# The lead-in of a lightning-attention and FFN kernel: both v cast by their transfers, w_in in other pieces, and the last block in three column pieces

## The chip, the cores and the metric

The kernel runs on one core of a Trainium2 chip. The metric is the device time of one execution in microseconds (us); the time of a version is the median of several executions. The engines are PE (matrix multiply, with PEld for its weight loads), DVE, ACT and POOL for element work, and SP, which issues transfers; POOL and ACT issue transfers too. The transfers run on 16 DMA engines that all queues share. PE writes to PSUM, 8 banks; DVE and ACT copy from there to SBUF.

## The reference

Decayed linear attention in blocks of 64 rows over (batch 4, heads 8, sequence 768, head size 64), and its output, as 3072 rows of 512, through a feed-forward part with g = h cos(h):

```python
for b in range(nb):
    intra = np.einsum('bhic,bhjc->bhij', qb, kb) * Dmask[None]
    intra = np.einsum('bhij,bhjd->bhid', intra, vb)
    inter = np.einsum('bhid,bhde->bhie', qb * lam_pow[None], kv_state)
    out[:, :, sl] = intra + inter
    kv_state = lam_block[None, :, None, None] * kv_state + np.einsum('bhsd,bhse->bhde', kb_dec, vb)
x = attn_out.transpose(0, 2, 1, 3).reshape(B * S, H * D)
h = x @ w_in             # 512 x 2048
out = (h * np.cos(h)) @ w_out   # 2048 x 512
```

Inputs and output are float32; the kernel multiplies in bf16.

## The kernel before

The 3072 rows are 24 blocks of 128 rows, taken in pairs, and grouped into tiles of the feed-forward part (`TILES`, line 21: 4, 2, 2, 2, 2, 2, 2, 4, 4 blocks). For each tile PE computes h by 16 column blocks f of 128 (`hidden`, line 702, matmuls at L705 into `ps_h`), ACT takes the cosine (L711), DVE multiplies (`gated`, L717) into `g`, and PE projects with w_out by groups of four f (`project`, L748 into `ps_f`); ACT copies the result (`project_out`, L762) and SP stores it (`store_out`, L769 and L771).

The attention of a tile is worked into the feed-forward part of the tile before. Only tile 0 has none before it: its four blocks are the **spans**, two stretches of 256 rows (x = 0 and 1), and their attention is the lead-in. `add_span` (line 545) makes it: q and k of a span are scaled (L559), transposed on PE (L570) and copied to SBUF by ACT (L573); scores on PE (L581), masked on DVE (L586); `update` (L595) makes the state between the span's two 128-row chunks, `update_out` (L599) copies it into `kv_bd`; `values` (L608) and `carried` (L614) make the output, which `values_out` (L622) copies into `xT`, the left operand of the first h. The masked scores come in two halves of heads (hp = 0 and 1).

Loads: `add_span_load` (line 272) brings q, k and v of a span. q and k come by SP as float32. v of span 0 comes by POOL's queue, whose transfers can change the type, so it arrives as bf16; it is issued once k of span 0 has landed. v of span 1 comes by SP as float32, once k of span 1 has landed, and POOL and ACT cast half of it each (`cast_v`, L563). The weights come by POOL's queue too, cast by their transfers: w_in in four pieces of 3, 5, 4 and 4 column blocks f (`W_IN`, line 37), then w_out in four pieces of four. `ORDER` (line 35) names the order; transfers of one queue are issued in it. The second w_in piece waits for the scaling of span 1's k, the fourth for the casts. The first loads of the blocks of tile 1 (q4 and on) wait on SP for the third w_out piece.

The order of all instructions on each engine comes from a planner (line 54): a greedy list schedule of tasks with durations, latencies, priorities and PSUM banks that are written at each task. At each step it takes the task that can start first, and among those on one engine the smallest priority. Its outcome is the fixed order of each engine's instructions, so an engine whose next instruction waits does nothing else meanwhile. In tile 0 the first `SPLIT` column blocks f (3) are done in two halves of 256 rows, so that h can begin on span 0 while span 1 is not ready; a task of the planner before `lead_end` is preceded by filler matmuls (`keep_awake`, L826) for the time that the plan shows PE idle.

The last block's projection (line 735) is done in two pieces of 256 columns; the first is copied by DVE and stored by SP, the second copied and stored by ACT.

Of the kernel before, what the change touches and what calls it, by code (L numbers as in the profile page):

```python
# [10 lines left out]
F32 = mybir.dt.float32  # L11
# [7 lines left out]
SPANS = 2  # L19
DMA_FROM = 6  # L20
TILES = [4, 2, 2, 2, 2, 2, 2, 4, 4]
SPLIT = 3
# [9 lines left out]
VALUES_OUT = [[("ACT",), ("ACT",)], [("ACT", "DVE"), ("ACT", "DVE")]]  # L32
STATE_OUT = [("ACT", "DVE"), ("ACT", "DVE")]
LATE = 30.0
ORDER = "q0 k0 q1 k1 v0 v1 i0 i1 i2 i3 o0 o1 o2 o3"

W_IN = [3, 5, 4, 4]
# [104 lines left out]
def kernel(  # L142
# [10 lines left out]
    nc = tc.nc  # L153
    B, H, S, D = q.shape
    P = 128
# [17 lines left out]
    BUFS = {"ld": 6, "qk": 3, "v_s": 6, "qkT": 3, "s_m": 4, "cos": 3, "o_sb": 3}  # L173
# [98 lines left out]
    def add_span_load(name, src, x, prio, deps):  # L272
        def emit(_):
            if on_pool:
                t = span_v[x]
            else:
                if ("raw", x) not in live:
                    live["raw", x] = work.tile([P, 3, H, 2, D], F32, tag="g", name="sp_f")
                t = live[name, "sp", x] = live["raw", x][:, "qkv".index(name[0])]
            return start(nc.gpsimd if on_pool else nc.sync, t.rearrange("u h s d -> u h (s d)"),  # L280
                         src[x, :, 0:2 * P, :].rearrange("h (u s) d -> u h (s d)", s=2), deps)

        on_pool = name == "v_f" and x == 0
        issue, load_t[name, "sp", x] = dma("POOL" if on_pool else "SP", 1.5, 1.0 if on_pool else 0.5, emit, prio, deps,
                                           lat=0.7 if name == "v_f" and x else 1.0)
        return load_t[name, "sp", x]
# [14 lines left out]
    def add_w(which, c, prio, deps=()):  # L301
        def emit(_):
            if which == "in":
                a, z = sum(W_IN[:c]) * P, sum(W_IN[:c + 1]) * P
                return start(nc.gpsimd, w_in_sb[:, :, a:z], w_in_src[:, :, a:z], deps)
            a, z = c * KF // WCH, (c + 1) * KF // WCH
            return start(nc.gpsimd, w_out_sb[:, a:z, :], w_out_src[:, a:z, :], deps)

        part = W_IN[c] / 4 if which == "in" else 1.0
        early = which == "in" and c < 2  # L310
        _, w_t[which, c] = dma("POOL", 2.68 * part, 0.8, emit, (-2000.0 if c == 0 else -997.5) if early else prio, deps,
                               lat=2.4 if early and c == 0 else 1.2)
        return w_t[which, c]
# [231 lines left out]
    def add_span(x):  # L545
# [16 lines left out]
        def cast_v(_, hp):  # L562
            (nc.scalar.copy if hp else nc.gpsimd.tensor_copy)(span_v[x][:, cut[hp]], live["v_f", "sp", x][:, cut[hp]])  # L563

# [24 lines left out]
        def update(t):  # L589
            kv_ps = L["kv"] = bank(t.bank[0], [P, NP, D], F32, "ps_kv")  # L590
            rows = chunks[0][0]
            for p in range(NP):
                for s in range(2):
                    for i, h in enumerate(halves):
                        nc.tensor.matmul(kv_ps[h, p, :], lhsT=L["k"][rows, s, 2 * p + i, :], rhs=L["v"][rows, s, 2 * p + i, :],  # L595
                                         start=(p == 0 and s == 0), stop=True, skip_group_check=True)

        def update_out(_, h, e):
            (nc.scalar.copy if e == "ACT" else nc.vector.tensor_copy)(kv_bd[h, x, :, h], L["kv"][h])  # L599
# [18 lines left out]
        def values_out(_, c, e, pairs):  # L618
            if ("xT", 0) not in live:
                live["xT", 0] = work.tile([P, KD, 4 * P], BF16, tag="xT", name="xT")  # L620
            n = 2 * x + c
            (nc.scalar.copy if e == "ACT" else nc.vector.tensor_copy)(  # L622
                live["xT", 0][:, pairs, n * P:(n + 1) * P], L["o"][c][:, pairs])

        so, kt, v_t = [[], []], [], [[load_t["v_f", "sp", x]]] * 2
        if x:

            v_t = [[pl.add(("POOL", "ACT")[hp], 0.61, [load_t["v_f", "sp", x]], partial(cast_v, hp=hp), pa(-1.0 + 0.1 * hp))] for hp in range(2)]
            w_t["in", 3].issue.deps += v_t[0] + v_t[1]
            late = w_t["in", 1].issue  # L630
        for hp in range(2):
# [3 lines left out]
            if x:  # L635
                late.deps.append(kt[hp])
            outs = []
            for name, src in (("qT", a), ("kT", kt[hp])):
                e = OUTS[x][name][hp]
                t = pl.add("PE", MM(P, 4), [src], partial(transposes, name=name, hp=hp), pa(-0.5 + 0.1 * hp), banks=1)  # L640
                if x and name == "kT" and hp == 0:
                    spans[0]["update"].deps.append(t)
                outs.append(pl.add(e, 0.58 if e == "ACT" else 0.42, [t], partial(transposes_out, name=name, hp=hp, e=e), pa(-0.5 + 0.1 * hp)))
                t.bank_frees = [[outs[-1]]]
            s1 = pl.add("PE", 0.42, outs, partial(scores, hp=hp), pa(0.1 + 0.1 * hp), banks=2)
            so[hp] = [pl.add("DVE", 0.69, [s1], partial(scores_out, hp=hp, i=i), pa(0.1 + 0.1 * hp + 0.05 * i)) for i in range(2)]
            s1.bank_frees = [[t] for t in so[hp]]

        u = pl.add("PE", 0.42, v_t[0] + v_t[1] + kt, update, pv(0.1), banks=1)
        L["update"] = u  # L650
        Uo_sp[x] = [pl.add(e, 0.4 if e == "ACT" else 0.42, [u], partial(update_out, h=h, e=e), pv(0.1))
                    for h, e in zip(halves, STATE_OUT[x])]
        u.bank_frees = [Uo_sp[x]]
        span_deps.extend(v_t[0] + v_t[1] + kt)
        v0 = pl.add("PE", 0.35, so[0] + v_t[0], partial(values, hp=0), pv(0.2), banks=2)
        v1 = pl.add("PE", 0.35, [v0] + so[1] + v_t[1], partial(values, hp=1), pv(0.25))
        second = pl.add("PE", MM(P, 4) + 0.1, [v1] + Uo_sp[x], carried, pv(0.3))
        for c, (t, by) in enumerate(zip((v1, second), VALUES_OUT[x])):
            cuts = [slice(i * NP // len(by), (i + 1) * NP // len(by)) for i in range(len(by))]
            Vo[2 * x + c] = [pl.add(e, 0.16 + 0.44 / len(by), [t], partial(values_out, c=c, e=e, pairs=pairs), pv(0.3) if c == 0 else -1200.0)  # L660
                             for e, pairs in zip(by, cuts)]
        v0.bank_frees = [Vo[2 * x], Vo[2 * x + 1]]

# [25 lines left out]
    def add_ffn(i):  # L689
# [43 lines left out]
        for j in range(nb):  # L733
            last = n0 + j == NBLK - 1
            pieces = [slice(0, DM // 2), slice(DM // 2, DM)] if last else [slice(0, DM)]
            store = None
            for piece, part in enumerate(pieces):
# [36 lines left out]
                eng, queue = ("DVE", "SP") if last and piece == 0 else ("ACT", "ACT" if last else "SP")  # L774
                e = pl.add(eng, 0.12 + width / 1060.0, [store], partial(project_out, eng=eng), begins[i + 1] + (j + 1) * nxt / nb,
                           get="o_sb")
                d = dma(queue, 1.2 if n0 + j < 2 * SPANS else 0.9, 1.7 if n0 + j < 2 * SPANS else 0.75, partial(store_out, eng=queue), n0 + j + 8, [e], ordered=False)[1]
# [9 lines left out]
    for at, name in enumerate(names):  # L787
# [5 lines left out]
        elif n < SPANS and at < 9:  # L793
            kept.append(add_span_load(which + "_f", src[which], n, at - 2040, {"v0": kept[1:2], "v1": kept[3:4]}.get(name, [])))
        else:
            kept.append(add_load(n, which + "_f", src[which], at, deps))
# [69 lines left out]
```

## Time and profile before

| | us |
|---|---|
| median of 5 executions | 208.92 (208.65 to 209.33) |
| the profiled execution | 208.77 |
| its span, first to last instruction | 207.1 |
| PE busy | 199.7 (96% of the span) |
| PE's granted clock, mean | 1.000 |
| DVE, ACT, POOL busy | 114.4, 119.0, 63.3 |
| v of span 0: issued, landed | 7.33, 12.5 |
| first w_in piece: issued, to landing | 8.40, 6.2 |
| v of span 1: issued, landed | 10.11, 16.1 |
| first h matmul | 15.60 |
| h without a break from | 19.98 |
| last ps_f matmul starts | 203.2 |
| last copy (ACT, 128x256) ends | 203.97 |

Times in the profile count from the first instruction. A row of a timeline or of the chain gives the start, the length, the engine, the line of the code and the operation, written as output<-inputs; "idle before <-" says how long the engine had been idle and what ended that. The chain of waits is followed back from the last instruction to what released it, so it shows what set the end, piece by piece. SPq, POOLq and ACTq rows are issues of transfers; their data moves later. What lies between the span and the execution's time (1.67 us) is outside the program's instructions.

### The profile page before, as it was taken

To read this page: it belongs to the slowest core of one execution; us is meant where nothing else is said; L and a number is where in the kernel's file an instruction comes from. 1 tells how busy PE (TensorE), PEld (TensorE's weight loads), DVE (VectorE), ACT (ScalarE), POOL (GpSimd) and SP (SyncE) were. 2 spreads that over 40 slices of the span, in tenths; PEclk is the share of its full clock that TensorE was granted. 3 is DMA by queue.
4 is the path that set the end of the run, shared out by engine and by line. 5 is a ranking of instruction groups with operands and counts; after the bars stand their busy time and mean duration, and the time that the engine had idled before them with its cause. 6 is when DMAs were issued, how large, how long until landed. Compare 5 with 4: busy or idle time off the path is not lost.

```text
span 207.1 us, 5989 instructions
## 1 busy us (share of the span) xinstructions
PE 199.7 (96%) x2498; PEld 117.6 (57%) x2498; DVE 114.4 (55%) x222; ACT 119.0 (57%) x231; POOL 63.3 (31%) x83
## 2 busy tenths in 40 slices
PE   6988999999999999999999999999999999999993
PEld 2456544555846857667667766655454444444462
DVE  2876686275972956647476664745784444444000
ACT  5865773233946867566659486746766555354120
POOL 4368001275055261546372363526200000000000
PEclk9999999999999999999999999999999999999999
DMA  4999999997889998999999999999500110111112
GB/s 126 293 218 199 208 206 200 215 258 182 191 200 208 216 247 207 225 184 260 225 251 156 225 232 218 207 205 247 131 3 3 51 51 0 54 51 51 51 77 75
DMA packets 95706, 34.20 MB, mean 165 GB/s; under 512 B 83264, under 2 KB 92736, under 8 KB 95680
## 3 DMA queue, kind: packets, MB, share of 16 engines
q1 hardware_dynamic: 90272, 29.24, 64.4%
q0 software_dynamic: 5264, 4.46, 13.7%
q8 instruction: 19, 0.31, 0.7%
q10 hardware_dynamic: 144, 0.13, 0.2%
q14 instruction: 7, 0.06, 0.1%
HBM read 27.27 MB, written 6.29 MB: 162 GB/s over the span
## 4 chain that ended last, share of the span: by engine, by line
PE 88%; DMA 6%; SPq 2%; DVE 1%; issue 1%; ACT 1%; POOL 0%; ACTq 0%
PE ps_h L705 40%; PE ps_f L748 40%; DMA sp_f<-in_v_dram 3%; DMA sp_f<-in_k_dram 3%; PE ps_o L475 2%; PE ps_kv L426 2%; PE ps_s L414 1%; PE ps_o L503 1%; SPq L266 1%; DVE v_s L344 1%; PE ps_t L366 0%; DVE xT L622 0%; ACT xT L622 0%; DVE qkT L369 0%; PE ps_o L608 0%
## 5 line engine op out<-in xcount | busy, mean ns | idle before, releaser
L717 DVE TENSOR_TENSOR g<-ps_h,cos 128x256 bf16<-128x256 f32 (+1 forms) x147 | 73.0, 506 | 57.7 <-ACT cos L711 57.0
L711 ACT ACTIVATE cos<-ps_h,halfpi 128x256 f32<-128x256 f32 (+1 forms) x147 | 75.4, 540 | 36.3 <-PE ps_h L705 36.1
L748 PE MATMUL ps_f<-w_out_sb,g 128*128 128x512 bf16 (+1 forms) x400 | 92.8, 371 | 0.0
L705 PE MATMUL ps_h<-xT,w_in_sb 128*128 128x256 bf16 (+1 forms) x588 | 92.4, 305 | 0.2 <-ACT xT L622 0.2
L705 PEld LDWEIGHTS <-w_in_sb 128*128 128x128 bf16 x588 | 57.1, 98 | 32.4 <-DVE xT L511 0.4
L748 PEld LDWEIGHTS <-g 128*128 128x128 bf16 x400 | 38.0, 98 | 35.7
L336 POOL TENSOR_TENSOR qk<-q_f,q_scale 128x512 bf16<-128x512 f32 x19 | 19.9, 1066 | 41.1 <-DMA q_f<-in_q_dram 31.3
L344 POOL TENSOR_TENSOR v_s<-v_f,v_scale 128x512 bf16<-128x512 f32 x19 | 19.6, 1042 | 16.2 <-DMA v_f<-in_v_dram 14.9
L762 ACT COPY o_sb<-ps_f 128x512 f32<-128x512 f32 (+1 forms) x24 | 13.9, 577 | 17.9 <-PE ps_f L748 17.5
L511 ACT CAST xT<-ps_o 128x512 bf16<-128x512 f32 x19 | 10.2, 588 | 15.6 <-PE ps_o L503 14.0
L419 DVE TENSOR_TENSOR s_m<-ps_s,mask 128x512 bf16<-128x512 f32 x20 | 12.9, 684 | 1.0 <-PE ps_s L414 0.7
L340 POOL CAST qk<-k_f 128x512 bf16<-128x512 f32 x18 | 11.0, 612 | 4.9 <-DMA k_f<-in_k_dram 4.7
L826 PE MATMUL ps_idle<-blank,ident 128*128 128x512 bf16 (+2 forms) x30 | 9.8, 457 | 1.6 <-POOL ident masks.py:199 1.6
L432 DVE TENSOR_TENSOR sum<-sum,ps_kv 128x512 f32<-128x512 f32 x15 | 10.2, 681 | 0.6
L437 ACT CAST S<-sum 128x512 bf16<-128x512 f32 x15 | 9.1, 619 | 2.5 <-DVE sum L432 2.4
L475 PEld LDWEIGHTS <-v_s 64*64 64x64 bf16 x320 | 4.2, 107 | 4.8 <-issue 4.6
L475 PE MATMUL ps_o<-s_m,v_s 64*64 64x64 bf16 x320 | 6.4, 197 | 0.5
L762 DVE COPY o_sb<-ps_f 128x256 f32<-128x256 f32 x1 | 0.4, 426 | 10.8 <-PE ps_f L748 10.8
L826 PEld LDWEIGHTS <-ident 128*128 128x128 bf16 x30 | 3.1, 116 | 4.8 <-issue 2.5
L586 DVE TENSOR_TENSOR s_m_sp<-ps_s,mask_sp 128x512 bf16<-128x512 f32 x8 | 5.0, 683 | 0.1
L426 PE MATMUL ps_kv<-v_s,qk 64*64 64x64 bf16 x288 | 4.8, 194 | 0.1
L340 ACT CAST qk<-k_f 128x512 bf16<-128x512 f32 x2 | 1.2, 618 | 6.3 <-DMA k_f<-in_k_dram 6.3
(71 smaller groups left out, 78.9 us busy)
## 6 DMA issues: line engine op xcount, KB each, us to landing
q_f<-in_q_dram SPq DMA_DIRECT2D x20, 256.0 KB, 4.2
k_f<-in_k_dram SPq DMA_DIRECT2D x20, 256.0 KB, 4.3
v_f<-in_v_dram SPq DMA_DIRECT2D x20, 256.0 KB, 4.6
out_dram<-o_sb SPq DMA_DIRECT2D x19, 256.0 KB, 2.6
w_out_sb<-in_moe_w_out_dram POOLq DMA_DIRECT2D x4, 512.0 KB, 13.5
out_dram<-o_sb SPq DMA_DIRECT2D x9, 128.0 KB, 2.4
sp_f<-in_q_dram SPq DMA_DIRECT2D x2, 512.0 KB, 5.3
sp_f<-in_k_dram SPq DMA_DIRECT2D x2, 512.0 KB, 5.6
```

Of the source, the lines that this page charges most:

```text
L336: vec[e].tensor_mul(new_qk()[:, 0, :, s], live.pop(("q_f", 2 * pr + s)), q_scale[:, c, :].unsqueeze(2).to_broadcast([P, H, D]))
L340: (nc.scalar.copy if early else nc.gpsimd.tensor_copy)(new_qk()[:, 1, :, s], live.pop(("k_f", 2 * pr + s)))
L344: vec[e].tensor_mul(live["v_s", 2 * pr + s], live.pop(("v_f", 2 * pr + s)), v_scale[:, c, :].unsqueeze(2).to_broadcast([P, H, D]))
L419: nc.vector.tensor_mul(t, live["s", pr][s], mask.unsqueeze(1).to_broadcast([P, H, D]))
L432: nc.vector.tensor_add(new, live["sum", pr, 0] if half else live["sum", pr - 1, 1], live["kv", pr][half])
L475: yield lambda h=h: nc.tensor.matmul(o[halves[h % 2], h // 2, m], lhsT=live["v_s", n0 + s][m, h, :], rhs=live["s_m", n0 + s][m, h, :], sta ...
L705: nc.tensor.matmul(t[:, :n], lhsT=w_in_sb[:, kd, f * P:(f + 1) * P], rhs=live["xT", i][:, kd, at], start=(kd == 0), stop=(kd == KD - 1))
L711: nc.scalar.activation(c[:, :n], live["h", i, f, at.start][:, :n], AF.Sin, bias=halfpi)
L717: nc.vector.tensor_mul(live["g", i][:, f, at], live.pop(("h", i, f, at.start))[:, :n], live.pop(("c", i, f, at.start))[:, :n])
L748: nc.tensor.matmul(live["f", i, j, piece][:, :width], lhsT=live["g", i][:, f, j * P:(j + 1) * P], rhs=w_out_sb[:, f, part], start=(f == 0) ...
L762: (nc.scalar.copy if eng == "ACT" else nc.vector.tensor_copy)(o[:, :width], live["f", i, j, piece][:, :width])
L826: nc.tensor.matmul(idle_ps[:, :n], lhsT=ident, rhs=blank[:, :n], start=True, stop=True)
```

## The change

Seven edits come together.

1. v of span 1 comes as v of span 0 does: by POOL's queue, cast by its transfer, without a wait of its own, in order behind v of span 0 and ahead of w_in. `cast_v` is gone, and the wait of a w_in piece for it.
2. w_in comes in five pieces of 2, 2, 4, 4 and 4 column blocks; the second still waits for the scaling of span 1's k.
3. `update` and the first `values` of span 0 stand behind span 1's first scores (before, `update` behind the transposes of its k).
4. `update` writes the two halves of heads into two PSUM banks; span 0's state is copied by ACT alone, span 1's by ACT and DVE. A chunk of span 1's output is copied whole, one by ACT and one by DVE, instead of each in two halves by both.
5. `SPLIT` is 4, and the planner's latencies of the early transfers are other numbers, so the whole plan is made anew.
6. The stores of tile 0 get a lower priority on SP, and there are four buffers `o_sb` instead of three.
7. The last block is projected in columns of 256, 128 and 128; the first two are copied by DVE and stored by SP.

```diff
-SPLIT = 3
+SPLIT = 4
-VALUES_OUT = [[("ACT",), ("ACT",)], [("ACT", "DVE"), ("ACT", "DVE")]]
-STATE_OUT = [("ACT", "DVE"), ("ACT", "DVE")]
+VALUES_OUT = [("ACT", "ACT"), ("ACT", "DVE")]
+STATE_OUT = [("ACT", "ACT"), ("ACT", "DVE")]
-ORDER = "q0 k0 q1 k1 v0 v1 i0 i1 i2 i3 o0 o1 o2 o3"
-W_IN = [3, 5, 4, 4]
+ORDER = "q0 k0 q1 k1 v0 v1 i0 i1 i2 i3 i4 o0 o1 o2 o3"
+W_IN = [2, 2, 4, 4, 4]
...
-    BUFS = {"ld": 6, "qk": 3, "v_s": 6, "qkT": 3, "s_m": 4, "cos": 3, "o_sb": 3}
+    BUFS = {"ld": 6, "qk": 3, "v_s": 6, "qkT": 3, "s_m": 4, "cos": 3, "o_sb": 4}
...
-        on_pool = name == "v_f" and x == 0
+        on_pool = name == "v_f"
         issue, load_t[name, "sp", x] = dma("POOL" if on_pool else "SP", 1.5, 1.0 if on_pool else 0.5, emit, prio, deps,
-                                           lat=0.7 if name == "v_f" and x else 1.0)
+                                           lat=1.6 if on_pool else 1.0)
...
-                               lat=2.4 if early and c == 0 else 1.2)
+                               lat=1.9 if early else 1.2)
...
-        def cast_v(_, hp):
-            (nc.scalar.copy if hp else nc.gpsimd.tensor_copy)(span_v[x][:, cut[hp]], live["v_f", "sp", x][:, cut[hp]])
...
-            kv_ps = L["kv"] = bank(t.bank[0], [P, NP, D], F32, "ps_kv")
+            L["kv"] = [bank(i, [P, NP, D], F32, "ps_kv") for i in t.bank]
...
-            w_t["in", 3].issue.deps += v_t[0] + v_t[1]
...
-                if x and name == "kT" and hp == 0:
-                    spans[0]["update"].deps.append(t)
...
+            if x and hp == 0:
+
+                for t in spans[0]["late"]:
+                    t.deps.append(s1)
...
-        u = pl.add("PE", 0.42, v_t[0] + v_t[1] + kt, update, pv(0.1), banks=1)
+        u = pl.add("PE", 0.42, v_t + kt, update, pv(0.1), banks=2)
...
+        L["late"] = [u, v0]
...
-            pieces = [slice(0, DM // 2), slice(DM // 2, DM)] if last else [slice(0, DM)]
+            cuts = [0, DM // 2, 3 * DM // 4, DM] if last else [0, DM]
+            pieces = [slice(a, z) for a, z in zip(cuts, cuts[1:])]
...
-                eng, queue = ("DVE", "SP") if last and piece == 0 else ("ACT", "ACT" if last else "SP")
+                eng, queue = ("DVE", "SP") if last and piece < 2 else ("ACT", "ACT" if last else "SP")
...
-                d = dma(queue, 1.2 if n0 + j < 2 * SPANS else 0.9, 1.7 if n0 + j < 2 * SPANS else 0.75, partial(store_out, eng=queue), n0 + j + 8, [e], ordered=False)[1]
+                d = dma(queue, 1.2 if n0 + j < 2 * SPANS else 0.9, 1.7 if n0 + j < 2 * SPANS else 0.75, partial(store_out, eng=queue), n0 + j + (26.5 if n0 + j < 2 * SPANS else 8), [e], ordered=False)[1]
...
-            kept.append(add_span_load(which + "_f", src[which], n, at - 2040, {"v0": kept[1:2], "v1": kept[3:4]}.get(name, [])))
+            kept.append(add_span_load(which + "_f", src[which], n, at - 2040, kept[1:2] if name == "v0" else []))
```

## The prediction, on record before the result

> **What bounds the kernel now.** I read four views in this order. First the busy table and the 40 slices of the page: PE is busy 96% of 207.1 us and its granted clock is full in every slice, so time is won only where PE is idle, does filler, or where the end comes after its last matmul. Second the chain of waits that ended last, in order of time (start, length, what):
>
> ```profile
> 4.11 5.98 DMA sp_f<-in_k_dram
> 10.11 6.01 DMA sp_f<-in_v_dram
> 16.11 0.06 issue
> 16.17 0.62 POOL v_sp L563
> ...
> 18.70 0.83 DVE xT L622 x2
> 19.55 0.38 ACT xT L622
> 19.98 12.69 PE ps_h L705 x64
> 32.67 0.63 PE ps_kv L672 x32
> 33.30 7.01 PE ps_f L748 x32
> 40.31 0.45 PE ps_t L366 x8
> ...
> 45.10 0.04 issue
> 45.15 0.44 PE ps_kv L426 x30
> ...
> 189.66 13.87 PE ps_f L748 x80
> 203.59 0.37 ACT o_sb L762
> ```
>
> The second span's v sets the lead-in: it lands at 16.11, is cast, goes through PE and leaves PSUM as xT at 19.92. From 19.98 to 203.6 the chain is PE nearly without a hole (0.6 us idle between 34 and 190 in the table by stages). A microsecond gained in the lead-in arrives at the end only if no later wait takes its place.
>
> Third the order of time of POOL's and SP's queues, and SP's waits:
>
> ```profile
> 7.33 1.08 POOL L266 DMA_DIRECT2D v_sp<-in_v_dram  x1 [3.67 <-DMA sp_f<-in_k_dram]
> 8.40 0.78 POOL L266 DMA_DIRECT2D w_in_sb<-in_moe_w_in_dram  x1
> 38.54 1.04 POOL L336 TENSOR_TENSOR qk<-q_f,q_scale 128x512 bf16<-128x512 f32 x1 [3.83 <-DMA q_f<-in_q_dram]
> SPq L266 <- DMA w_out_sb<-in_moe_w_out_dram: 22.9, 1, 22.9
> ```
>
> The last line matters most: the loads of tile 1 (q4 and on) wait on SP for the third w_out piece, which lands at 33.34. So the weights' stream on POOL's queue dates both the weights and tile 1's loads.
>
> Fourth the packet records and landings of the DMA engines. Landings in us: k1 10.09, v0 12.51, w_in 0 14.56, v1 16.11, w_in 1 to 3 20.63, 23.18, 25.78, w_out 28.31, 30.81, 33.34, 35.94. The engines served these in order of issue: v1, issued on SP at 10.11, has no packet before 13.7, when w_in 0 is nearly through. From 9 to 36 us they are never free, so a place gained by one transfer is lost by another.
>
> **The transfers after the change.** v0 stays (12.51). v1 is issued behind it at 8.4 on POOL, without waiting. It has 1024 packets that write 256 B, as v0; v0's went at 440 per us, so 2.33 us: last packet at 12.23+2.33=14.56, landing 0.28 later, **14.84** instead of 16.11. The two casts (L563, 0.61 us) go too: v1 is usable 1.9 us sooner. The price: as f32 by SP its 1024 packets went at 678 per us, 1.51 us, so the stream is 0.8 us longer.
>
> w_in 0 and 1 are now two column blocks each: 512 packets that write 512 B, which no row shows. Neighbours: 256 B 36 ns per packet and engine, 768 B 67 ns, 1024 B 80 ns. I take the middle, 52 ns (bounds 36 and 67): 32 packets per engine, 1.66 us (1.16 to 2.13). w_in 0 lands at **16.5** (16.0 to 17.0), two us later than now; w_in 1 at 18.2 (17.2 to 19.1). One more term: during w_in 1 the 16 engines' landings spread from 0.8 to 1.95 us, one of them carrying a 16 KB instruction packet of 0.95 us. Nothing says where this falls now: 0 to 1.2 us, I take 0.3, so w_in 1 at **18.5**. Each further piece is 2.53 us (distance of the landings above): w_in 2 at 21.0, third w_out piece at 33.7, 0.35 later than now (bounds 32.4 to 35.5).
>
> POOL: v0 1.08, v1 1.08, w_in 0 0.78 from 7.33 ends at 10.27; the k preps behind started at 10.26 (k1 lands at 10.09). Nothing. w_in 1 and later are issued from 12.3 as now; the two later ones no longer wait for the casts (16.72), but their descriptors queue behind earlier pieces anyway: nothing.
>
> **PE in the lead-in.** Second span's scores first: update and values of span 0 now stand behind scores that need POOL's k prep (11.34), transposes and an ACT copy (0.58), so they start near 13.0 instead of 12.55. Costs nothing: what follows waits for v1 and w_in. It frees DVE earlier: the masked scores of span 1 end near 15.6 instead of 16.42. Both halves of span 0's state on ACT add 0.37 there; xT of span 0 is ready near 15.3 (now 15.22), covered by w_in 0 at 16.5. Two banks let ACT and DVE copy span 1's state side by side (now 17.39 then 17.77, 0.4 saved), also before w_in 0: nothing by itself.
>
> So w_in sets the pace. By the planner's order of earliest starts the h of f0 and f1 for blocks 0 and 1 come ahead of the last values of span 1, so PE idles from about 15.5 to 16.5, does these 8 matmuls (0.109 each, rows at 15.6: 0.87), values and carried (0.6, to 18.1), and xT's last chunk leaves on DVE near 19.0 (0.69 row at L511). Then f2, f3 on w_in 1: 18.5+0.87 (with SPLIT 4 four f are cut in halves); the four second halves 16 x 0.109=1.74, to 21.1, when w_in 2 (21.0) is there; 48 matmuls of 512 columns x 0.216=10.37, to **31.5**. The same sum for before, 19.98 + 12 x 0.109 + 52 x 0.216, gives 32.5 where the chain shows 32.67; with that 0.1 the h phase ends at 31.6, **1.1 us sooner**. Bounds: 1.45 sooner (xT at 19.05 is then the limit) to 0.75 later (w_in 1 at 20.3).
>
> The idle microsecond on PE: the trace's first matmuls of 512 columns are 427 ns apart, from 1.6 to 6 us, and 216 later; no row has PE idle for a microsecond after that. A fall of the clock would cost by that row up to half of 4.4 us; I take nothing, as the 0.6 us of idle before 19.98 cost none. The Trainium skill ("TensorE: Matmul & The Clock Gate", Part 1) has the clock fall after an idle window of about 3.4 us; by that this wait costs nothing. The filler of L826 is placed in planned gaps and costs at most one matmul, 0.2, where PE waits anyway.
>
> **What is late next.** Tile 1's first transposes (40.31) need q5's prep, POOL at 38.54+1.04=39.58: 0.6 us of slack. q5 comes 0.35 later, so 40.0 with the semaphore. PE would be there 1.1 sooner, but a planner that fills gaps has one more group of four ps_f ready (0.865): 31.6+0.63+9 x 0.865=40.0. No wait; without the ninth group 0.9, made good later by that group. ps_kv at 45.15 has no slack: DVE's v_s took 1.45 beside POOL. Now it ends near 45.0 with 13 groups done instead of 12: gain there 0.15+0.865=1.0. For small new waits in a replanned middle I take 0.2 off: **lead-in -0.8**. Later pairs are issued 4 us and more ahead of their scores (transposes at 106.5 for scores at 117). Stores of tile 0 at lower priority and a fourth o_sb move SP's order near 46 to 62, where PE waits for nothing: nothing, and 0.3 at risk if a load of pair 4 is later.
>
> **The end.** Now: last matmul starts 203.24, copy 128x256 on ACT 203.60 to 203.97, issue 204.00, landing 205.71, then 1.3 of closing. After: 32 matmuls of 128 columns for 16 of 256: rows at L570, L614 and L366 start 56 ns apart with a weight load each, 32 x 0.056=1.79 against 16 x 0.109=1.74: +0.05; the last one's tail is 219 instead of 273 ns, -0.05. The copy: ACT 0.585 at 512 and 0.37 at 256 columns, so 0.265 at 128: -0.11. The store: 1.98 for 256 KB and 1.68 for 128 KB on SP, so about 0.12 less. The middle piece, on DVE and SP, is done 0.9 earlier. **End -0.2** (-0.3 to +0.05). The skill's page named above (Part 2, back-to-back issue gap) gives 81 ns for a sustained stream of 128 columns with its weight loads; by that, an estimate, the matmuls are 2.6 us and the end is 0.6 later. The rows have only up to 8 in a run.
>
> **Sum.** The profiled execution took 208.77 (span 207.1 and 1.67 around it): 208.77-0.8-0.2=207.8. Its time is 0.15 under the median of the runs: forecast **207.9**.
>
> **Rivals.** *Forecast, 0.50*, 207.4 to 208.4. *All of it arrives, 0.16*: 512 B packets near 36 ns, no lag; -1.45 and -0.2: 207.3. For it: the 256 B row; against: w_in 1's spread. *The weights eat it, 0.17*: third w_out piece at 34.8 (1.4 late), packets near 67 ns with some lag. Then w_in 1 is at 19.6, the h phase ends where it does now, q5's prep at 41.0, and only the end's 0.2 and at most 0.2 more remain: 208.6. That the change doesn't do what it says is its near kin: v1 first means w_in 0 later, one wait for another. *Slower, 0.17*: the same stream at the far bounds. w_in 1 at 20.3 puts the h phase 0.75 later, tile 1's loads start at 35.5 and ps_kv loses 0.8; less 0.2: 209.5. It decides from a third w_out piece later than about 35.1. For it: v as casts is slower than as f32 in this trace; against: it takes both bounds together.
>
> Under 0.2% (0.4 us) a change can't be told from none in this kernel. Faster: 0.16+0.46 of the forecast =0.62; same: 0.04 of it and 0.16 of the third case =0.20; slower: 0.17 and the third's last 0.01 =0.18. The range, 207.0 to 209.3, leaves out the outer ends of the first and last case.
>
> **What would show it.** L563 gone; v1 landing by 15; PE waiting for w_in 0 near 16.5 and w_in 1 near 18.5; ps_h's end near 31.6; SP's load of q4 near 33.7; ps_t within 0.3 of 40.0; last ACT copy 0.27 and landing about 0.2 sooner after the last matmul. Wrong: w_in pieces at other distances, L705 waiting for w_in 2, PE idle between 34 and 60 above 0.6, or PE idle later where the replanned order brings new waits.

## The result, and the profile after

| | before | after |
|---|---|---|
| median, us | 208.73 (54 executions) | 208.15 (30 executions) |
| lowest, us | 208.08 | 206.85 |
| the profiled execution, us | 208.77 | 207.09 |
| its span, us | 207.1 | 205.4 |

The ratio after to before is 0.9959, with a 95% interval of 0.9945 to 0.9974: **0.9 us faster** (0.5 to 1.1). It compares fast executions alone, without the six of after that took 210.1 us or more; the medians of all differ by 0.6. The profiled execution is one of the best of its kernel, 1.1 us under its median. So two things have to be explained: the 1.7 us of this execution, and why most others have less.

The changed code stands up to eight lines earlier: L705 is now L697, L748 L741, L672 L664, L608 L605, L614 L611, L595 L592, L762 L755, L769 L762, L771 L764, L826 L819.

The chain of waits of after between 12 and 50 us (start, length, what):

```profile
11.28 1.00 POOL k_sp L559
12.28 0.75 POOL w_in_sb L266
13.03 7.43 DMA w_in_sb<-in_moe_w_in_dram
20.47 0.05 issue
20.51 10.97 PE ps_h L697 x52
31.48 0.63 PE ps_kv L664 x32
32.11 7.88 PE ps_f L741 x36
39.98 0.45 PE ps_t L366 x8
...
47.78 0.97 PE ps_f L741 x4
48.75 1.35 PE ps_h L697 x12
```

The second span's v, its cast and xT are gone from the chain; the third w_in piece (landing at 20.47) stands there now. The h phase ends at 31.48 instead of 32.67, tile 1's transposes start at 39.98 instead of 40.31 with nine groups of ps_f done instead of eight, and tile 1's h starts at 48.75 instead of 50.20. From there to the first instruction of the last block both kernels need the same time, within 0.1 us.

PE in the order of time, where h begins (last bracket: idle before, and what ended it):

```profile
15.88 0.41 PE L605 MATMUL ps_o<-s_m_sp,v_sp 64*64 64x128 bf16 x15
16.65 0.21 PE L605 MATMUL ps_o<-s_m_sp,v_sp 64*64 64x128 bf16 x1 [0.36 <-issue]
16.80 0.61 PE L697 MATMUL ps_h<-xT,w_in_sb 128*128 128x256 bf16 x4
17.24 0.39 PE L611 MATMUL ps_o<-qT_sp,kv_bd 128*128 128x128 bf16 x4
17.47 2.80 PE L697 MATMUL ps_h<-xT,w_in_sb 128*128 128x256 bf16 x24
20.51 3.85 PE L697 MATMUL ps_h<-xT,w_in_sb 128*128 128x512 bf16 x19 [0.24 <-DMA w_in_sb<-in_moe_w_in_dram]
```

The first w_in piece had landed at 15.20 and the second at 17.87; neither is waited for. What the start of h waits for is the one matmul at 16.65: PE stands still in front of it for 0.57 us from start to start (0.36 of it idle), with all its data there ("issue": nothing that the profile shows). From 16.80 the h phase is dense but for 0.24: 32 matmuls of 0.109, 48 of 0.216 and the carried part's 0.3 are 14.2, plus 0.24 and 0.3 at the edges gives the 31.48. Those 0.24 are the wait for the third w_in piece, so in this execution it is that piece, and not the stop, that sets the end of the h phase: with a shorter stop PE would have waited longer for it.

The kernel before has the same kind of stop, at 17.99, between two matmuls of the values of span 1:

```profile
17.08 0.55 PE L608 MATMUL ps_o<-s_m_sp,v_sp 64*64 64x128 bf16 x23
17.99 0.30 PE L608 MATMUL ps_o<-s_m_sp,v_sp 64*64 64x128 bf16 x7 [0.36 <-issue]
```

The end of after (the two rows of DVE are the first two pieces, ACT and its queue the last):

```profile
200.19 0.42 DVE L755 COPY o_sb<-ps_f 128x256 f32<-128x256 f32 x1 [10.70 <-PE ps_f L741]
200.64 1.15 SPq L764 DMA_DIRECT2D out_dram<-o_sb  x2
201.14 0.29 DVE L755 COPY o_sb<-ps_f 128x128 f32<-128x128 f32 x1 [0.52 <-PE ps_f L741]
202.02 0.27 ACT L755 COPY o_sb<-ps_f 128x128 f32<-128x128 f32 x1 [2.99 <-PE ps_f L741]
202.31 0.37 ACTq L764 DMA_DIRECT2D out_dram<-o_sb  x1
```

From the last block's first matmul of 256 columns to the last landing it is 5.75 us instead of 5.85.

### The profile page after: what moved, and what is told of

It is laid out like the page before. It is cut to its first block, busy times and chain, and to the rows that moved or that the text cites. A ratio compares the mean times of both kernels' runs of the same rounds, so it can differ in the third digit from the quotient of the medians.

```text
span 205.4 us, 6027 instructions
## 1 busy us (share of the span) xinstructions
PE 199.0 (97%) x2516; PEld 118.1 (57%) x2516; DVE 113.3 (55%) x222; ACT 119.1 (58%) x231; POOL 64.0 (31%) x84
## 4 chain that ended last, share of the span: by engine, by line
PE 88%; DMA 7%; SPq 2%; POOL 1%; issue 0%; ACT 0%; POOLq 0%; ACTq 0%
PE ps_f L741 41%; PE ps_h L697 39%; DMA w_in_sb<-in_moe_w_in_dram 4%; DMA sp_f<-in_k_dram 3%; PE ps_o L475 2%; PE ps_kv L426 2%; PE ps_s L414 2%; PE ps_o L503 1%; SPq L266 1%; POOL k_sp L559 1%; PE ps_t L366 0%; POOL w_in_sb L266 0%; PE ps_kv L664 0%; SPq L185 0%; ACT o_sb L755 0%
## 5 line engine op out<-in xcount | busy, mean ns | idle before, releaser
L697 PE MATMUL ps_h<-xT,w_in_sb 128*128 128x256 bf16 (+1 forms) x592 | 92.3, 304 | 0.2 <-DMA w_in_sb<-in_moe_w_in_dram 0.2
L741 PE MATMUL ps_f<-w_out_sb,g 128*128 128x512 bf16 (+2 forms) x416 | 92.5, 363 | 0.0
L697 PEld LDWEIGHTS <-w_in_sb 128*128 128x128 bf16 x592 | 57.1, 98 | 32.0 <-issue 0.7
L741 PEld LDWEIGHTS <-g 128*128 128x128 bf16 x416 | 38.5, 98 | 35.7
L755 ACT COPY o_sb<-ps_f 128x512 f32<-128x512 f32 (+1 forms) x24 | 13.7, 572 | 23.9 <-PE ps_f L741 23.9
L819 PE MATMUL ps_idle<-blank,ident 128*128 128x512 bf16 (+3 forms) x28 | 9.6, 469 | 1.6 <-POOL ident masks.py:199 1.6
L755 DVE COPY o_sb<-ps_f 128x256 f32<-128x256 f32 (+1 forms) x2 | 0.7, 358 | 11.2 <-PE ps_f L741 11.2
L819 PEld LDWEIGHTS <-ident 128*128 128x128 bf16 x28 | 2.9, 118 | 4.6 <-issue 2.5
L671 POOL CAST S<-sum 128x512 bf16<-128x512 f32 x1 | 0.6, 609 | 14.7 <-DVE sum L668 14.7
```

The costliest lines, as they stand in the source:

```text
L697: nc.tensor.matmul(t[:, :n], lhsT=w_in_sb[:, kd, f * P:(f + 1) * P], rhs=live["xT", i][:, kd, at], start=(kd == 0), stop=(kd == KD - 1))
L741: nc.tensor.matmul(live["f", i, j, piece][:, :width], lhsT=live["g", i][:, f, j * P:(j + 1) * P], rhs=w_out_sb[:, f, part], start=(f == 0) ...
L755: (nc.scalar.copy if eng == "ACT" else nc.vector.tensor_copy)(o[:, :width], live["f", i, j, piece][:, :width])
L819: nc.tensor.matmul(idle_ps[:, :n], lhsT=ident, rhs=blank[:, :n], start=True, stop=True)
```

## The experiments

Each ratio is to the kernel before, run beside it on the same chip. "Tile 1's h" is the start of its first matmul in the profiled execution (before 50.1, after 48.6): from it to the start of the last matmul each of these executions takes 153.0 to 153.3 us, and what PE waits or loses in the middle comes on top.

| run | ratio, 95% interval | tile 1's h | profiled execution |
|---|---|---|---|
| again | 0.9985, 0.9957 to 1.0013 | 50.0 | 208.8 |
| end_two_pieces | 0.9975, 0.9950 to 1.0000 | 48.8 | 208.7 |
| before_v_cast | 0.9963, 0.9937 to 0.9989 | 52.1 | 210.2 |
| before_v_cast_end_three | 0.9981, 0.9949 to 1.0012 | 49.9 | 208.2 |
| w_in_3544 | 0.9974, 0.9952 to 0.9996 | 50.1 | 208.6 |
| filler_128 | 0.9983, 0.9961 to 1.0005 | 49.0 | 209.2 |
| before_filler_128 | 1.0027, 1.0012 to 1.0042 | 51.0 | 209.6 |
| few_fillers | 0.9980, 0.9959 to 1.0001 | 50.2 | 208.6 |
| filler_128_w_in_2233 | 0.9964, 0.9945 to 0.9983 | 49.1 | 208.0 |
| stores_as_before | 1.0058, 1.0020 to 1.0095 | 49.0 | 211.5 |
| stores_as_before_filler_128_w_in_2233 | 1.0058, 1.0021 to 1.0095 | 49.2 | 209.9 |
| priority_alone | 0.9994, 0.9962 to 1.0025 | 48.6 | 207.4 |

Most of these intervals are 0.4 to 0.6% wide: the versions differ less than executions of one version do. The traces say more than the ratios, except where an interval stands clear of the others, as with the two runs whose stores are undone.

**The change once more**, unaltered, as the measure of how far a repeat strays.

> The changed kernel once more, to see how much of the profile on record repeats. Theory (the lead-in carries the gain): 0.6 to 1.1 us under the kernel before; in the profile v of span 1 lands near 13.8, the h phase of tile 0 ends between 31.3 and 32.0 (before 32.67), and the last block, from its first 256-column matmul to the last landing, takes 5.75 us (before 5.85). Rival (the profile on record was a lucky execution and the lead-in gives nothing lasting): the h phase ends at 32.4 or later in this profile.

Its profiled execution has a lead-in that is hardly shorter than before's: h starts at 18.44 and ends at 32.62. The same matmul, with the same data long there, is 1.6 us later (v of span 1 had landed at 13.51):

```profile
15.89 0.41 PE L605 MATMUL ps_o<-s_m_sp,v_sp 64*64 64x128 bf16 x15
18.30 0.21 PE L605 MATMUL ps_o<-s_m_sp,v_sp 64*64 64x128 bf16 x1 [1.99 <-issue]
18.44 0.61 PE L697 MATMUL ps_h<-xT,w_in_sb 128*128 128x256 bf16 x4
```

The rival's sign, an h phase that ends at 32.4 or later, is met in this execution, and the ratio can't be told from none. So one and the same kernel has a tile 1's h at 48.6 or at 50.0, and this stop makes the difference. The traffic of the transfer engines between 14 and 17 us shows two things that differ, first in after, then in the repeat (packets, MB, share of the 16 engines' time; packets overlap, so a share can pass 100%):

```profile
q0 software_dynamic: 816, 0.46, 115.8%
q8 instruction: 1, 0.02, 2.0%
```

```profile
q0 software_dynamic: 712, 0.41, 113.2%
q8 instruction: 1, 0.02, 4.5%
```

The weights' queue (q0) moved fewer packets in the repeat. The other line is one 16 KB packet of PE's instructions (after has 20 of them for 5032 recorded matmuls and weight loads): 2.0% of 16 x 3 us is 0.95 us, 4.5% is 2.1 us. By the packet records it starts at 14.46 in after and at 14.80 in the repeat, so it ends at 15.41 and 16.94; PE goes on at 16.65 and 18.30, 1.24 and 1.36 later.

**The end**, back in two pieces.

```diff
-            cuts = [0, DM // 2, 3 * DM // 4, DM] if last else [0, DM]
+            cuts = [0, DM // 2, DM] if last else [0, DM]
...
-                eng, queue = ("DVE", "SP") if last and piece < 2 else ("ACT", "ACT" if last else "SP")
+                eng, queue = ("DVE", "SP") if last and piece == 0 else ("ACT", "ACT" if last else "SP")
```

> The change with the last block in two pieces of 256 columns again. Theory: the end is worth 0.1 us, so 0.1 over the changed kernel and still 0.7 under the kernel before. Rival (the end is the larger part): 0.4 or more over the changed kernel.

0.9975 against 0.9959 fits the 0.10 us of the two profiles (0.05%) and can't tell it from nothing. What the profile shows beside it is where a gained lead-in goes. Tile 1's h starts at 48.8, as early as in after, and yet the span is 207.0, because PE waits in the middle. The largest waits of PE:

```profile
PE ps_s L414 <- DMA qkT<-qk: 1.8, 2, 1.0
...
PE ps_o L605 <- issue: 0.6, 1, 0.6
```

The scores of a later pair (L414) wait for its transposes, which SP issues behind loads and stores. I measured the margin from the landing of a pair's second transpose to its first score, in pairs 3 to 11. Before: 1.8 to 4.2 us. After, in its good execution: 0.1, 1.2, 1.2, 1.9, 2.8, then 1.6 and more. In this run: 0.2, 0.8, 0.05, 0.05, 0.6, 0.05, 1.6, 0.2, 0.06 (at 0.05 PE starts as the transposes land; two of these are waits of 1.04 and 0.72). In w_in_3544, whose tile 1 starts as late as before's: 1.6 and then 2.4 or more. PE came earlier, the loads and transposes did not: a second chain, of transfers, stands close behind PE. It does not follow from the earlier lead-in alone: priority_alone, below, starts tile 1 as early and has 1.8 and more where the records show it.

**v of span 1 cast by its transfer, alone**: the kernel before with the first edit.

```diff
-        on_pool = name == "v_f" and x == 0
+        on_pool = name == "v_f"
...
-            v_t = [[pl.add(("POOL", "ACT")[hp], 0.61, [load_t["v_f", "sp", x]], partial(cast_v, hp=hp), pa(-1.0 + 0.1 * hp))] for hp in range(2)]
-            w_t["in", 3].issue.deps += v_t[0] + v_t[1]
...
-            kept.append(add_span_load(which + "_f", src[which], n, at - 2040, {"v0": kept[1:2], "v1": kept[3:4]}.get(name, [])))
+            kept.append(add_span_load(which + "_f", src[which], n, at - 2040, kept[1:2] if name == "v0" else []))
```

> The kernel before with one part of the change alone: v of span 1 cast by its transfer, on POOL's queue behind v of span 0; w_in stays 3, 5, 4, 4, SPLIT 3. Theory (an early v is what gains, its rate behind a transfer of its own queue is near 690 packets per us): v lands near 13.8, the first w_in piece near 15.9, the second near 19.5 to 20.1, the h phase ends at 31.0 to 31.6, the time is 0.8 to 1.2 under the kernel before. Rival (v first only puts w_in later): h phase not before 32.4, no gain.

0.9963: as good as the whole change, within the intervals. Its profiled execution (210.2) is a bad one, and shows one way to an execution above 210; of the six executions of after above 210, three had a granted clock of 0.998 or more, so there are other ways. PE's stop is 1.97 here, until 18.82, and then the granted clock falls. Busy time by stretches (us from:to; length; busy time of PE, PEld, DVE, ACT and POOL, each with its count of instructions; the granted clock; the transfer engines' busy share; GB/s):

```profile
16.84:18.82 1.98, 0.23 (x16) 0.06 (x7) 0.57 (x2) 0.37 (x1) 0.99 (x2) 1.00 1.16 200
18.82:19.76 0.94, 0.94 (x11) 0.83 (x11) 0.00 (x0) 0.12 (x1) 0.00 (x0) 1.00 1.25 209
19.76:23.17 3.41, 3.41 (x19) 2.35 (x17) 1.91 (x5) 2.11 (x5) 0.00 (x0) 0.50 1.24 209
```

PE is busy and gets half the clock for 3.41 us, which costs 1.7 by estimate (half of it).

**The same with the last block in three pieces**: before with the first and the seventh edit.

> The kernel before with two edits alone: v of span 1 cast by its transfer in POOL's queue ahead of w_in, and the last block in columns of 256, 128 and 128. It has w_in in pieces of 3, 5, 4, 4, SPLIT 3, the stores as before. Theory (the first of the seven edits brings most of the gain, through v and through margins that stay at 2.5 us and more; the end brings 0.1; the other edits bring little): ratio 0.9945 to 0.9965, first h near 17, h end at 31.5 to 32.4 where the clock does not fall, no wait for a transposed qkT between 60 and 150 us. Rival (the smaller first pieces of w_in and the second span's scores first are needed): w_in 0 near 17 delays h, h end at 32.5 or later, ratio 0.998 to 1.0.

0.9981, the interval reaching from 0.9949 to 1.0012. Nothing but the stop disturbs its profile: it lasts until 18.03 (1.49), h runs from 18.21 to 32.58, no wait in the middle, span 206.5. It is 0.6 below before's span: 0.3 of it in the lead-in, 0.2 at the end, the rest in between. Its margins are 1.0 to 3.4 us, not 2.5 and more. The first w_in piece (16.33) is hidden by the stop. So neither the theory that the first edit brings all nor its rival is decided by the ratio; the trace says that with w_in in pieces of 3, 5, 4, 4 the stop sets h, as in the repeat of the change.

**w_in in its old pieces**, all else as in the change.

```diff
-W_IN = [2, 2, 4, 4, 4]
+W_IN = [3, 5, 4, 4]
```

> The change with w_in in pieces of 3, 5, 4, 4 again. Theory (the pieces of w_in set PE's pace once v is early): the third column block's neighbour f3 comes with the second piece near 19.5 to 20.1, PE stands at f3 of the first half before it goes on to the second halves, and the h phase ends 0.6 to 1.2 later than in the changed kernel, so the time is that of the kernel before within 0.4. Rival (only v's place matters): within 0.2 of the changed kernel.

h starts at 17.61 and waits 0.5 for the second piece (21.17), so the h phase ends at 32.56, 1.1 later than in after. The ratio is 0.9974 all the same; that whole margins of the transposes make up for it is argued, not shown. The pieces are worth 1.1 us in the lead-in of these two executions and 0.3 in the ratios, within their intervals.

**PE's filler, in matmuls of 128 columns**: more instructions for the same time, so that the stop comes earlier in time, where PE waits anyway; in the change, and in before.

```diff
-            n = min(cols, 4 * P)
+            n = min(cols, 2 * P if at < 7.0 else P)
```

> The change with its filler matmuls cut narrower (256 columns before 7 us of the plan, 128 after, instead of up to 512): the same filler time in 53 more matmuls, 106 more rows on PE. Theory (in every profile so far PE stops at its 449th row, near 16.1 in the change, until 1.2 to 1.5 us after a 16 KB instruction packet has ended; the packet is asked for at a fixed earlier row, and waits behind data): that row now comes some 100 rows earlier in the work, near 14 us, and the asking some us earlier, so the stop at the last values of span 1 (0.4 to 2.2 us) goes; first h near 16.2, h phase ends at 31.0 to 31.6 in any profile, median 0.9 to 1.7 under the kernel before, with a smaller spread than the change. Rival (PE waits there for POOL, a bank or a semaphore): the stop stays at the same matmul with the same length, the time stays that of the change.

> The kernel before with the same narrower fillers, 120 rows more. Theory (before, v of span 1 at 16.1 set the lead-in and its stop at row 449, 0.4 to 0.6 us, was mostly beside other waits): the stop at 17.4 goes, but ACT and DVE copies still end xT near 19.5: median 0 to 0.4 under the kernel before. Rival (instruction packets alone set the lead-in, v's place is nothing): as large a gain as in filler_128.

A row here is a matmul or a weight load. In every run above, PE stops in front of the same row: the 448th recorded, or the 446th where two records are missing (the expectations count one more and call it the 449th). With 106 more rows of filler PE stops in front of the 448th again, now at 14.72 and in `carried`; its packet starts at 12.95:

```profile
14.60 0.34 PE L611 MATMUL ps_o<-qT_sp,kv_bd 128*128 128x128 bf16 x3
15.19 0.22 PE L611 MATMUL ps_o<-qT_sp,kv_bd 128*128 128x128 bf16 x1 [0.25 <-issue]
```

So the stop goes with the count of instructions and not with the matmul, against the rival. h ends at 31.27 (31.41 in after, on the same timeline), after a wait of 0.20 for the third w_in piece. The gain is lost on the spot and later: ps_f now waits for the third w_out piece, and scores for transposes. The ratio, 0.9983, misses the theory's 0.9 us and more.

```profile
PE ps_s L414 <- DMA qkT<-qk: 1.5, 2, 0.8
PE ps_f L741 <- DMA w_out_sb<-in_moe_w_out_dram: 0.4, 1, 0.4
```

In before the stop lies at 15.06 in the filler, but there v of span 1 lands at 16.95 in that execution; h ends at 33.47, and the ratio, 1.0027, is slower: neither the theory (0 to 0.4 us faster) nor the rival holds.

**Hardly any filler**: none after 6.5 us, 34 rows fewer.

```diff
-            keep_awake((t.start - now) * 0.95 if now < 2.0 else t.start - now, now)
+            if now < 6.5:
+                keep_awake((t.start - now) * 0.95 if now < 2.0 else t.start - now, now)
```

> The change without its fillers after 6.5 us of the plan: 34 rows fewer on PE. Theory: the 449th row now lies 34 rows later in the work, among the h matmuls near 17.5 to 18, and the packet is asked for only some 0.2 us later, so the stop is about 1.2 us shorter, mostly 0: h phase ends at 31.2 to 32.0, median 0.6 to 1.4 under the kernel before, unless PE's idle stretches now halve its granted clock for a stretch of 3.4 us (then 1.7 us more in such executions). Rival (fillers are needed to keep the clock): clock halved in the profile or most executions, at or over the kernel before.

The stop is not there. The packet ends at 15.59, and PE, with half the clock, comes to its 448th row only at 18.7: three microseconds later, with nothing to wait for. That is what a cause by the packet asks for. The clock halves here too, after two stretches without a start of 1.13 and 0.82 us, and does so in 10 of 12 executions:

```profile
10.00:13.40 3.40, 1.81 (x56) 1.25 (x48) 2.56 (x5) 2.17 (x5) 3.19 (x4) 1.00 1.68 171
13.40:16.80 3.40, 3.40 (x101) 2.86 (x101) 2.61 (x5) 2.16 (x5) 3.40 (x6) 0.50 1.16 143
```

It costs little here: h starts at 16.80 as in after. That the h phase ends only at 32.39 comes from the transfers: w_in lands at 18.28 and 21.45 for its second and third piece (17.87 and 20.47 in after), and h waits for both, 0.26 and 0.81.

**Short filler and w_in in pieces of 2, 2, 3, 3, 3, 3.**

> filler_128 with w_in in six pieces of 2, 2, 3, 3, 3, 3. Theory (without the instruction stop PE next waits for the third w_in piece, 20.47 in the profile of the change, by 0.25 to 0.5 us): the third piece with three blocks instead of four is 0.5 us sooner and PE doesn't wait: 0.2 to 0.4 under filler_128. Rival (that wait is hidden or the smaller packets cost as much as they save): within 0.15 of filler_128.

0.9964, and a narrow spread (207.07 to 208.64, clock 0.997 or more in all 12): 0.4 us under filler_128 as the theory had it, but the intervals overlap. No wait for w_in; the stop is 0.97 from start to start, most of which PE would have waited for v of span 1 (it lands at 15.51 here); one wait for transposes is left (0.5). It does not beat the change.

**The stores' priority.** The sixth edit undone, in the change and in the run just shown.

```diff
-    BUFS = {"ld": 6, "qk": 3, "v_s": 6, "qkT": 3, "s_m": 4, "cos": 3, "o_sb": 4}
+    BUFS = {"ld": 6, "qk": 3, "v_s": 6, "qkT": 3, "s_m": 4, "cos": 3, "o_sb": 3}
...
-                d = dma(queue, 1.2 if n0 + j < 2 * SPANS else 0.9, 1.7 if n0 + j < 2 * SPANS else 0.75, partial(store_out, eng=queue), n0 + j + (26.5 if n0 + j < 2 * SPANS else 8), [e], ordered=False)[1]
+                d = dma(queue, 1.2 if n0 + j < 2 * SPANS else 0.9, 1.7 if n0 + j < 2 * SPANS else 0.75, partial(store_out, eng=queue), n0 + j + 8, [e], ordered=False)[1]
```

> The change with its sixth edit undone: the stores of tile 0 have their old priority on SP and o_sb has three buffers again. Theory (in the change the stores of tile 0 stand between loads of later pairs on SP, and this, with the earlier lead-in, eats the margin between the landing of a pair's transposes by SP and its scores): the margin of the fourth pair rises from 0.1 to 0.2 us back to 1.5 to 2.4, PE does not wait for a transposed qkT between 60 and 150 us, first transposes of tile 1 still at 39.9 to 40.4 and the end of the h phase at 31.4 to 31.7 where PE's stop at its 449th instruction is short; ratio to the kernel before 0.9935 to 0.9965, at or under that of the change. Rival (margins are small because PE is earlier, wherever the stores stand): margins of 0 to 1 us at the fourth to sixth pair as in the change, some waits of 0.5 to 1 us, ratio 0.996 to 0.9985 as its repeats.

> The steadiest of the versions so far (w_in in pieces of 2, 2, 3, 3, 3, 3 and fillers of 128 columns; 0.9964) with the sixth edit undone. Theory (the stores' place on SP takes the margin): the wait for the transposed qkT near 70 us (0.75) goes, and the ratio is 0.9925 to 0.995. Rival (the margin goes with PE's earlier start): the wait stays at 0.5 to 1 us, ratio 0.9955 to 0.9975.

Both theories fall, and in the other direction: 1.0058, **2.1 us slower** than the change (1.0% of 208.7 between the two ratios), slower than before too. The waits for transposes are gone, as the theories said, and the lead-in is 0.4 us behind the change's; the loss is one other wait. PE of stores_as_before in order of time:

```profile
56.08 0.45 PE L414 MATMUL ps_s<-qkT 64*64 64x64 bf16 x32
56.35 0.20 PE L426 MATMUL ps_kv<-v_s,qk 64*64 64x64 bf16 x2
58.56 0.44 PE L426 MATMUL ps_kv<-v_s,qk 64*64 64x64 bf16 x30 [2.01 <-POOL v_s L344]
58.93 4.45 PE L741 MATMUL ps_f<-w_out_sb,g 128*128 128x512 bf16 x12
```

and SP's queue ahead of it, with the v load that POOL's v_s needs:

```profile
44.28 0.92 SPq L266 DMA_DIRECT2D v_f<-in_v_dram  x1
45.31 4.55 SPq L762 DMA_DIRECT2D out_dram<-o_sb  x6
49.96 2.75 SPq L372 DMA_TRANSPOSE qkT<-qk  x2
52.76 0.58 SPq L266 DMA_DIRECT2D v_f<-in_v_dram  x1
```

The second block's v stands behind six stores and two transposes, is issued at 52.76 instead of 44.58 (after) or 44.50 (before, with the same priorities as here), and lands at 57.40. The replanned order, not the chip, made this: with the new start times the greedy planner found the stores ready first. The place alone is not enough: in before_v_cast_end_three the same v is issued at 52.24, lands at 55.73, and PE doesn't wait. And in this execution the wait is paid twice, since the clock falls a microsecond after it:

```profile
56.50:58.60 2.10, 0.09 (x11) 0.04 (x8) 1.95 (x4) 0.63 (x2) 1.13 (x2) 1.00 0.76 172
58.60:59.70 1.10, 1.10 (x34) 0.69 (x34) 0.66 (x1) 0.00 (x0) 1.10 (x2) 0.98 1.05 239
59.70:63.10 3.40, 3.40 (x10) 1.03 (x7) 0.71 (x2) 1.24 (x2) 2.17 (x4) 0.50 0.99 233
```

12 matmuls of 512 columns take 4.45 us here instead of 2.6. The clock was below full in 4 of 12 executions of this run (median 211.5, the others 209.6) and in 7 of 12 of the other (211.5 and 209.9).

**Its two halves**: the low priority kept, o_sb back to three buffers.

> The change with the second half of its sixth edit undone: the stores of tile 0 keep their low priority on SP, o_sb has three buffers. By the plan SP then issues both k and v of the fifth pair's loads ahead of the fourth store of tile 0, and PE's order is that of the change. Theory (the priority alone keeps the v loads of the fourth pair ahead of the stores, which is what spared the 2 us wait at 56): no wait of ps_kv for v_s near 56 us, tile 1's first transposes at 39.8 to 40.4, ratio to the kernel before 0.994 to 0.998, as the change. Rival (the fourth buffer is needed): copies of tile 0 wait for a buffer, PE waits for a PSUM bank between 48 and 62 us for 0.4 us or more, ratio 0.9985 or higher.

The wait at 56 is not there, nor one for a PSUM bank, and the profiled execution has tile 1's h at 48.6 and a span of 205.5, as after. So the priority is the half that spares this wait. The ratio, 0.9994, is in the rival's range though the waits that the rival names are not there, and its interval reaches from the change's value past none; what the fourth buffer is worth stays open.

## Why the prediction was right, and which steps were off

The forecast was 207.9 with faster as the likely sign; 208.15 was measured. That the sum came out so near is in part luck: the profiled execution gained 1.7 us, more than the 1.0 forecast, its repeat none, and the median lies between for reasons that the forecast had at nothing. By parts:

- **The h phase 1.1 sooner, ps_t at 40.0 behind a ninth group, tile 1's h gaining 1.0:** in the profiled execution 1.19, 39.98, nine groups, and 1.45 (predicted 0.15 + 0.865, by ps_kv; v_s was done by DVE in 0.68 instead of 1.52, so that ps_kv no longer waits). The numbers hold; that h waits for w_in 0 and 1, from which they were worked out, does not.
- **v1 at 14.84:** it landed at 13.80. The rate taken from v0, 440 packets per us, contains a start of about 0.7 us with nearly no packets, after SP's transfers end. Behind another transfer of its own queue v1 went at 690 per us. It landed 1.44 us behind v0, where it took 1.51 as float32: the 0.8 booked as the price in the stream was none.
- **w_in 0 at 16.5, h waiting for it:** 15.20, and no wait. 512 B packets took 42 ns per packet and engine, not 52; w_in 1 came 2.67 behind it instead of 2.0, by the spread of the landings, which got 0.3; it was at 17.87 (18.5). w_in 2 at 20.47 (21.0) is the only one waited for, 0.24; the prediction had PE and this piece arrive together (21.1 and 21.0), and that held.
- **The step that failed is what sets h.** "So w_in sets the pace", by pieces 0 and 1: what holds up the start of h is PE's stop at its 448th row, and where it is long it sets the end too; where it is short, as in after, the third piece does. Before's trace had the stop, from 17.42 to 17.99 between two values matmuls, inside the stretch that the prediction put down to v as a whole. The stop is 0.57 in after and priority_alone, 1.41 in stores_as_before, 2.21 in the repeat (start to start), and it is the first part of what other executions have less than the best one.
- **"Nothing later" (later pairs are issued 4 us and more ahead):** wrong as a rule. Margins of 0.04 to 1.2 us are common in pairs 3 to 8 of the versions with the earlier lead-in, and four of the profiled executions wait 0.3 to 1.8 us there. I had counted from the issue of the transposes, not from their landing, and not in the new order. This is the second part.
- **1.67 around the span, taken as it was:** a third part. In before it is 1.79 at most in the 111 executions measured beside these runs. In the six versions with the last block in three pieces and the filler not made shorter or fewer (after, again, before_v_cast_end_three, w_in_3544, stores_as_before, priority_alone) 32 of 90 executions have more than 1.80 outside the span, up to 2.54; in the other seven versions none of 80. In four of the six profiles a 20th packet of instructions starts 0.4 to 1.0 us after the span's end (205.77 in after), and in no other profile does one come so late; that it is the cause is not shown.
- **Idle on PE costs nothing:** true for the waits of 0.2 to 0.6 us, not for 2. Two of the 30 executions of after had the clock at 0.992 or less (210.25 and 212.5 us). That the lower bound for it was taken as the value is the error; the row used (0.6 us idle) reached no further.
- **The stores of tile 0, "nothing, and 0.3 at risk":** the step mis-sized most, though it cost nothing. With the sixth edit undone they cost 2.1.
- **The end, -0.2:** 0.10. The matmuls came 56 ns apart over 32 of them, the copy took 0.27, as predicted; the last store of 64 KB took 1.68 instead of 1.71, so the 0.12 set on it was 0.03.

Of the rivals, "all of it arrives" (207.3) is what single executions do (206.85 at best), and "one wait for another" is what the repeat does. The change's median lies between them; the stop, the margins and the time outside the span differ from one execution to the next, and how much each takes of the median is not shown. That the packet causes the stop is shown by place and time, not by taking it away: in thirteen of the fourteen profiled executions the stop is in front of the same row, whatever stands there, and PE goes on 1.24 to 1.48 us after the packet's end, with ends from 13.9 to 17.4; in the fourteenth, few_fillers, PE comes 3 us after the packet and does not stop. What makes the packet late by one microsecond or by three stays open.

## What to carry to other kernels

When a lead-in is full of transfers, count what else uses them: PE's instructions come through the same engines here, and for a stop labelled "issue" at a fixed count of instructions, look whether a packet of theirs has just landed. Before a gain in the lead-in is booked, measure the margin of every later chain from its landing to its use, in the new order; one with less margin than the gain can take the rest. And when a hand-prioritised planner gets new start times, compare the order on each queue before and after: a small priority can be what keeps a load ahead of stores.

## What the runs showed of the hardware

- In thirteen of fourteen profiles PE stops in front of its 448th recorded row (the 446th where two records are missing) for 0.5 to 2.2 us, while the transfer engines are full. The 16 KB packet of instructions starts 1.4 to 3.6 us after PE has passed the row 256 places earlier (12.78 and 14.46 in after, 12.56 and 15.81 in before_v_cast_end_three) and takes 0.9 to 1.3 us, 2.1 once. The packets later in the same profiles (at 20.4 and 34.5 in after) are followed by no such stop.
- The Trainium skill ("Runtime: NRT & Kernel Launch", Instruction fetch mechanics) says that instructions come in blocks of 16 KiB, 256 each, and that the cost of crossing a block is mostly hidden. The block agrees with the packet; "hidden" does not hold for this first stop, of up to 2.2 us; it does for the later packets.
- The granted clock halved for 3.41 us after stops of about 2 us (before_v_cast, stores_as_before), and after two of 1.13 and 0.82 with 0.2 between (few_fillers; start to start); it set in 0.9 to 1.1 us after PE was busy again. Not every such stop brought it: after 2.21 us in the repeat, and after a wait of 2.2 in stores_as_before_filler_128_w_in_2233, the clock stayed full. In the kernel before none of the 111 executions measured beside these runs had it.
- The Trainium skill ("TensorE: Matmul & The Clock Gate", Part 1) gives an idle window of about 3.4 us for the fall, free-running. The halved stretch has that length here; the idle before it was shorter.
- The matmuls of 128 columns in the last block, 32 of them with their weight loads, start 56 ns apart. The 81 ns that the Trainium skill ("TensorE: Matmul & The Clock Gate", Part 2) gives for a sustained stream was not seen over this many.
